# The last three token tiles of a fused attention, routing and MLP kernel in another order

## The chip, the core and the metric

The kernel runs on one core of one Trainium2 chip. The metric is the device time of one execution in microseconds (us). Before the change the median of three runs is 432.23 us (431.24 to 432.95).

## What is computed

Three stages follow one another in one launch. The first is a linear attention with decay over 2 x 768 tokens, 8 heads of 48 channels; its result is 1536 rows of 384. The second sends each row to the one of 8 experts with the largest gate logit, at most `capacity` rows each, and multiplies what the expert returns by a gate weight. The third is a dense MLP. Cut to what matters:

```python
state = w * state + k_t v_t^T                 # per head, token by token
y_t   = r_t @ (state_before + u * k_t v_t^T)
e     = argmax(x @ w_gate);  pos = rank of the token within its expert
disp[e, pos] = x                              # if pos < capacity
y     = relu(disp @ w1[e]) @ w2[e];  out = gate_w * y[e, pos]
g     = h * clip(h + 3, 0, 6) / 6,  h = out @ w_in;  result = g @ w_out
```

The gate weight is folded into the rows before they are dispatched (`sm` scales `x`), so a row is scaled once and then written to its expert's place.

## The kernel before

**Stages.** `attention()` (lines 242 to 886) walks 12 tiles of 128 tokens; `moe()` (line 897) walks the 8 experts, each with 224 columns of rows; `mlp()` (line 1084) walks blocks of 384 tokens. fp32 products of the two later stages are made of three products of a high and a low part: weights are cast to a high part on ScalarE (`high`, line 188) and the low part is a subtraction (`low`, line 194).

**Order.** The scheduler is manual: each engine runs its instructions in the order in which the Python code issues them, and semaphores join the engines. The small steps of the routing of a tile stand in a list `todo`; `tick(n)` issues the next n of them on VectorE (with a ScalarE or GpSimd instruction inside some), `ranks(0)` issues the rank products on TensorE, `gate(t)` the logits, `turn(t)` three transposes on TensorE and the copy `xT` on ScalarE that `gate` reads, `values(t, i)` eight products, `finish_x(t, i)` the addition on VectorE (line 435) that completes half of a tile's rows, `bonus(t)` eight scalings on ScalarE (line 429) that this addition needs.

**Routing of a tile** (`route`, line 588): maximum, one-hot, exponent; then `ranks`; sum and reciprocal (`inverse`, line 616), the position, and `done` (line 639). Tiles 9, 10 and 11 (`t >= LATE`) do not go through DRAM for expert 0: their rows are put into expert 0's tile by products with a selection matrix. For that `inverse` makes a high part `lasth` on ScalarE (line 620), a low part `lastl` is made by VectorE (line 632, tiles 9 and 11) or GpSimd (line 625, tile 10), and `done` makes the selection `first` (line 642). `late_rows(t)` (line 677) then issues six products: three with the high part, three with the low part. All three tiles are also scattered to DRAM by an indirect DMA of GpSimd (`spread`, line 702) for the other experts; `fetch(e)` (line 234) reads an expert's rows back and waits for all the scatters before it.

**Zero products.** `keep_warm(n, bank)` (line 254) issues n bf16 products of a tile of zeros, 128x384; nothing reads them.

**The end of the stage** (lines 828 to 886) is written out by hand: tile 11's attention, the routing of tiles 9, 10 and 11 interleaved, 12 products that bring expert 0's fetched rows `xr` into the same PSUM tiles (line 877), `late_rows`, and then `moe()` begins with `turn(0)`, whose copies `xh` (line 923) start expert 0's first products (line 995). In the iteration for tile 10 the piece of expert 0's weights that covers its second half is cast on ScalarE by `high(slice(0, PC))` (line 820).

Of the kernel before, what the change touches and what calls it, by code (L numbers as in the profile page):

```python
# [8 lines left out]
F32 = mybir.dt.float32  # L9
F32R = mybir.dt.float32r  # L10
# [3 lines left out]
ALU = mybir.AluOpType  # L14
# [51 lines left out]
def kernel(  # L66
# [175 lines left out]
    def attention():  # L242
        actx = ExitStack()
        with actx:
# [159 lines left out]
            def carried(T):  # L404
                py_t[T] = [
                    (bank(2 + i, "py") if T < NTILE - 1 else bank("a", "py"))[:, :DM].rearrange(
                        "p (n i d) -> p n i d", n=NP, i=2
                    ) for i in range(2)
                ]
                if T % CB:  # L410
                    for p in range(NP):
                        for i in range(2):
                            nc.tensor.matmul(  # L413
                                py_t[T][i][:, p], head(rT[T], i)[:, p, :],
                                head(Z[T], i)[:, p, :].unsqueeze(1).to_broadcast([D, 2, D]),
                                start=p == 0, stop=False,
                            )
# [8 lines left out]
            def bonus(T):  # L426
                x_t[T] = xq.tile([P, DM], F32, tag="x", name="x")
                for h in range(H):
                    nc.scalar.activation(
                        x_t[T][:, h * D:(h + 1) * D], v_of(T)[:, h % 2, h // 2, :], AF.Copy, scale=dg[T][:, h]  # L430
                    )
# [29 lines left out]
            def turn(T):  # L461
                pt = bank("tr", "pt")[:, :DM].rearrange("p (k t) -> p k t", k=KD)
                for k in range(KD):
                    nc.tensor.transpose(pt[:, k, :], x_t[T][:, k * P:(k + 1) * P], ident)  # L464
                xT = p2.tile([P, KD, P], F32, tag="xT", name="xT", bufs=1)
                nc.scalar.copy(xT, pt)
                xT_t[T] = xT
# [21 lines left out]
            def ranks(age=1):  # L489
                if todo and isinstance(todo[0][0], list):  # L490
                    age_, mm = todo[0][0]
                    if age_ >= age:
                        todo[0].pop(0)
                        mm()
                    else:
                        todo[0][0][0] += 1
# [91 lines left out]
            def route(t):  # L588
                if t < GRP * NGRP:
                    if t % GRP == GRP - 1:  # L590
                        route_group(t - GRP + 1)
                    return
                last, tail = t >= LATE, t == NTILE - 1
                pl = lgt.pop(t)
                l, po = pl[:, 0:E], pl[:, 64:64 + 2 * E]
                rk, pe = pl[:, 192:192 + E], pe_all[:, t, :]
                oh = oh_all[:, t, :]
                oh2 = oh.unsqueeze(1).to_broadcast([P, 2, E])
                slot = slots[:, t:t + 1]
                V = nc.vector  # L600
                mx = p2.tile([P, 1], F32, tag="mx", name="mx")
                d = p2.tile([P, E], F32, tag="d", name="d")
                m2 = p2.tile([P, 1], F32, tag="m2", name="m2")
                sm = p2.tile([P, 1], F32, tag="sm", name="sm", bufs=4)
                sel = p2.tile([P, 2, E], F32, tag="sel", name="sel")
                sf = p2.tile([P, 1], F32, tag="sf", name="sf")

                def diff():
                    V.tensor_tensor(out=d, in0=l, in1=mx.to_broadcast([P, E]), op=ALU.subtract)
                    nc.scalar.activation(gex[:, t % GRP, 0:E], d, AF.Exp)  # L610

                def rank_mm():
                    base_mm(po, t, True, False)
                    nc.tensor.matmul(po, tri, oh2, start=False, stop=True)

                def inverse():
                    V.reciprocal(sm, sm)
                    if last:
                        hi = lastp.tile([P, DM], F32R, name=f"lasth{t}")
                        nc.scalar.activation(hi, x_t[t], AF.Copy, scale=sm)  # L620
                        last_h[t] = hi
                        if t == NTILE - 2:
                            nc.scalar.activation(x_t[t], x_t[t], AF.Copy, scale=sm)
                            lo = lastp.tile([P, DM], F32R, name=f"lastl{t}")
                            nc.gpsimd.tensor_tensor(out=lo, in0=x_t[t], in1=hi.bitcast(F32), op=ALU.subtract)
                            last_l[t] = lo

                def low_rows():
                    o = first[t]
                    if t != NTILE - 2:  # L630
                        lo = lastp.tile([P, DM], F32R, name=f"lastl{t}")
                        V.scalar_tensor_tensor(
                            out=lo, in0=xs_t[t], scalar=sm, in1=last_h[t].bitcast(F32), op0=ALU.mult, op1=ALU.subtract
                        )
                    else:
                        lo = last_l[t]
                    first[t] = ((last_h[t], o), (lo, o))

                def done():
                    if last:  # L640
                        o = lastp.tile([P, WIN], F32R, name=f"first{t}")
                        V.tensor_scalar(
                            out=o, in0=col, scalar1=sf, scalar2=None, op0=ALU.is_equal
                        )
                        first[t] = o
                        xs_t[t] = x_t[t]
                        last_ops[t] = [low_rows]
                    V.tensor_scalar(out=slot, in0=sf, scalar1=float(FAR), scalar2=None, op0=ALU.add)
                    if t == NTILE - 2:
                        ready.append((slot, x_t.pop(t)))  # L650
                    else:
                        scat.append((slot, x_t.pop(t), sm))

                todo.append([
                    lambda: V.tensor_reduce(out=mx, in_=l, axis=AX.X, op=ALU.max),
                    lambda: V.scalar_tensor_tensor(
                        out=rk, in0=l, scalar=mx, in1=rank, op0=ALU.is_equal, op1=ALU.mult
                    ),
                    diff,
                    lambda: V.tensor_reduce(out=m2, in_=rk, axis=AX.X, op=ALU.max),  # L660
                    lambda: V.tensor_tensor(out=oh, in0=rk, in1=m2.to_broadcast([P, E]), op=ALU.is_equal),
                    [0, rank_mm],
                    lambda: V.tensor_reduce(out=sm, in_=gex[:, t % GRP, :], axis=AX.X, op=ALU.add),
                    inverse,
                    lambda: V.tensor_tensor(
                        out=sel, in0=po.rearrange("p (a e) -> p a e", a=2), in1=oh2, op=ALU.mult
                    ),
                    lambda: V.tensor_reduce(out=pe.unsqueeze(2), in_=sel, axis=AX.X, op=ALU.add),
                    lambda: V.tensor_scalar(
                        out=sf, in0=pe[:, 0:1], scalar1=cap_f, scalar2=pe[:, 1:2], op0=ALU.is_lt, op1=ALU.mult  # L670
                    ),
                    done,
                ])

# [72 lines left out]
            for T in range(NTILE - 1):  # L747
# [69 lines left out]
                    rest = low  # L817
                if T == 10:
                    high, low = begin(hi_only=True)
                    high(slice(0, PC))  # L820
                finish_x(T, 0)
                finish_x(T, 1)
                if T == 10:
# [8 lines left out]
            fetch(0)  # L832
            load_to(7)
            T = NTILE - 1
            carried(T)
            bonus(T)
            values(T, 0)
            ranks(0)
            turn(T - 1)
            finish_x(T, 0)  # L840
            drain(0)
            values(T, 1)
            gate(T - 1)
            finish_x(T, 1)
            load_to(8)
            keep_warm(2, 0)
            route(T - 1)
            tick(3)
            turn(T)
            tick(2)  # L850
            finish(T - 2)
            late_rows(LATE, 0)
            keep_warm(2, 0)
            ranks(0)
            keep_warm(3, 0)
            tick(5)
            gate(T)
            route(T)
# [10 lines left out]
            tick(2)  # L869
            drain(0)  # L870
            finish(T)
            scale()
            scatter()
            keep_warm(3, 0)
            for n in range(2 * KD):
                k, c = divmod(n, 2)
                nc.tensor.matmul(
                    px0[k][:, c * P:min(WIN, (c + 1) * P)], xr[:, c, k * P:(k + 1) * P],
                    ident[:, :min(P, WIN - c * P)], start=False, stop=False,
                )  # L880
            late_rows(LATE + 1)
            late_rows(T)
            scatter()
            scale(nc.vector)
            scatter()
            late.extend((lambda: rest(nc.vector, slice(HC, PC)), lambda: low(nc.vector)))
# [549 lines left out]
```

## Time and profile before

| | |
|---|---|
| median of 3 runs | 432.23 us (431.24 to 432.95) |
| the profiled execution | 431.22 us |
| its span, first to last instruction | 429.4 us |
| mean granted TensorE clock over the span | 0.985 |
| TensorE busy | 416.0 us (97%), 3159 products |
| VectorE / ScalarE / GpSimd busy | 251.8 / 204.1 / 177.0 us |
| first product of the experts (line 995) | 90.28 us after the start |

The profiled execution has its own time; the 1.8 us between it and the span lie ahead of the first and behind the last instruction. Times of rows are counted from the start of the span. A granted clock of 1.00 is 2.4 GHz and 0.50 is 1.2 GHz.

### The profile page before, as it was taken

How to read it: one execution, taken by the hardware profiler on the slowest of the kernel's cores; microseconds unless marked ns; L12 is line 12 of the kernel's file. 1: busy time of each engine (PE TensorE's matmuls, PEld its weight loads, DVE VectorE, ACT ScalarE, POOL GpSimd, SP SyncE). 2: the span in 40 equal slices, each digit the busy share in tenths (PEclk: the TensorE clock that was granted, in tenths of full speed). 3: DMA queues.
4: the chain of work that ended last, by engine and by line, in shares of the span. 5: the costliest groups of instructions: out<-in, count | busy, mean ns of one | idle time of the engine just before them, and what ended most of it. 6: DMA issues, size and time to landing. Idle time of an engine off the chain costs nothing.

```text
span 429.4 us, 8115 instructions
## 1 busy us (share of the span) xinstructions
PE 416.0 (97%) x3159; PEld 403.1 (94%) x3159; DVE 251.8 (59%) x473; ACT 204.1 (48%) x434; POOL 177.0 (41%) x146
## 2 busy tenths in 40 slices
PE   7999999899999999999999999999999999999992
PEld 4799999799999999999999999999999999999992
DVE  5998988598986767775978779670313122130310
ACT  2374677556636656658436254352505134250520
POOL 4875685126567467567000000001625226160441
PEclk9999999699999999999999999999999999999997
DMA  7987999646198899898622511001010000100001
GB/s 225 234 272 265 334 338 393 226 143 279 50 288 255 195 352 255 198 358 211 232 76 73 173 65 60 0 2 55 2 37 20 0 2 0 56 1 2 0 21 44
DMA packets 17361, 62.20 MB, mean 145 GB/s; under 512 B 2912, under 2 KB 7136, under 8 KB 17312
## 3 DMA queue, kind: packets, MB, share of 16 engines
q1 hardware_dynamic: 13024, 54.27, 40.1%
q0 software_dynamic: 1968, 4.73, 3.1%
q10 hardware_dynamic: 2320, 2.57, 1.8%
q8 instruction: 27, 0.44, 0.4%
q14 instruction: 22, 0.18, 0.1%
HBM read 53.70 MB, written 7.87 MB: 143 GB/s over the span
## 4 chain that ended last, share of the span: by engine, by line
PE 85%; issue 6%; POOL 2%; DMA 2%; DVE 2%; ACT 1%; SPq 0%; POOLq 0%; DVEq 0%; ACTq 0%
PE psh L1113 20%; PE pso L1136 19%; PE psm L995 15%; PE pym L1030 6%; PE pym L1034 6%; PE py L421 4%; PE pym L1031 3%; PE psa L394 2%; PE pl L475 2%; DMA hTt<-in_hT_dram 2%; PE py L413 2%; POOL gl L1102 2%; PE pt L464 1%; PE pu L442 1%; PE px L913 1%
## 5 line engine op out<-in xcount | busy, mean ns | idle before, releaser
L1117 DVE SCALAR_TENSOR_TENSOR g<-g,psh 128x384 f32<-128x384 f32 x64 | 35.3, 552 | 98.8 <-ACT g L1116 98.4
L1116 ACT ACTIVATE g<-psh,three 128x384 f32<-128x384 f32 x64 | 37.2, 582 | 73.3 <-PE psh L1113 73.3
L1102 POOL TENSOR_TENSOR gl<-g,gh 128x384 fp32r<-128x384 f32 x40 | 40.3, 1012 | 51.1 <-ACT gh L1101 51.1
L1154 POOL DMA_INDIRECT out_dram<-o,cid x12 | 11.8, 980 | 116.2 <-ACT o L1152 107.9
L1030 PE MATMUL pym<-h,wbh 128*128 128x448 f32 x120 | 38.3, 377 | 0.0
L194 POOL TENSOR_TENSOR wal<-raw,wah 128x1536 fp32r<-128x1536 f32 x7 | 24.6, 3517 | 24.4 <-ACT wah L188 12.9
L1101 ACT CAST gh<-g 128x384 fp32r<-128x384 f32 x64 | 32.3, 505 | 3.5 <-DVE g L1117 3.5
L1001 ACT ACTIVATE h<-psm 128x448 fp32r<-128x448 f32 x32 | 17.5, 547 | 32.3 <-PE psm L995 31.6
L1113 PE MATMUL psh<-y2l,wbh 128*128 128x384 f32 x96 | 32.4, 337 | 0.0
L1113 PE MATMUL psh<-y2l,wah 128*128 128x384 f32 x96 | 32.4, 337 | 0.0
L1113 PE MATMUL psh<-y2h,wah 128*128 128x384 f32 x96 | 32.3, 336 | 0.0
L1113 PE MATMUL psh<-y2h,wbh 128*128 128x384 f32 x96 | 32.3, 336 | 0.0
L1113 PE MATMUL psh<-y2h,wbl 128*128 128x384 f32 x96 | 32.1, 335 | 0.0
L1113 PE MATMUL psh<-y2h,wal 128*128 128x384 f32 x96 | 32.1, 335 | 0.0
L1136 PE MATMUL pso<-wah,gh 128*128 128x384 f32 x96 | 32.1, 334 | 0.0
L1136 PE MATMUL pso<-wbh,gh 128*128 128x384 f32 x96 | 32.1, 334 | 0.0
L1136 PE MATMUL pso<-wbh,gl 128*128 128x384 f32 x96 | 32.1, 334 | 0.0
L1136 PE MATMUL pso<-wal,gh 128*128 128x384 f32 x96 | 32.1, 334 | 0.0
L1136 PE MATMUL pso<-wah,gl 128*128 128x384 f32 x96 | 32.1, 334 | 0.0
L1136 PE MATMUL pso<-wbl,gh 128*128 128x384 f32 x96 | 32.1, 334 | 0.0
L995 PE MATMUL psm<-xh,wah 128*128 128x224 f32 x192 | 31.9, 275 | 0.1
L995 PE MATMUL psm<-xh,wal 128*128 128x224 f32 x192 | 31.7, 275 | 0.0
(192 smaller groups left out, 1143.6 us busy)
## 6 DMA issues: line engine op xcount, KB each, us to landing
raw<-in_w_dram SPq DMA_DIRECT2D x32, 768.0 KB, 8.2
tokt<-in_tok_dram SPq DMA_DIRECT2D x12, 576.0 KB, 4.7
raw<-in_w_in_dram SPq DMA_DIRECT2D x8, 768.0 KB, 5.0
raw<-in_w_out_dram SPq DMA_DIRECT2D x8, 768.0 KB
hTt<-in_hT_dram SPq DMA_DIRECT2D x12, 448.0 KB, 5.6
xs<-zero SPq DMA_DIRECT2D x8, 384.0 KB
xr<-xs ACTq DMA_DIRECT2D x6, 384.0 KB, 7.6
xr<-xs SPq DMA_DIRECT2D x2, 384.0 KB, 3.2
```

The lines of the kernel that those rows point to most:

```text
L194: eng.tensor_tensor(out=lo[:, sl][:, h], in0=raw[:, h], in1=hi[:, sl][:, h].bitcast(F32), op=ALU.subtract)
L421: nc.tensor.matmul(py_t[T][i][:, p], A_t[T % 2][:, i, p, :], v_of(T)[:, :, p, :], start=T % CB == 0 and p == 0, stop=p == NP - 1,)
L995: nc.tensor.matmul(ps[:, fi, :], wa_tile(a, k, 2 * q + fi), b[:, k, :], start=n == k == 0 and not (both and fi), stop=n == 2 and k == KD - ...
L1001: nc.scalar.activation(hh, ps, AF.Relu)
L1030: nc.tensor.matmul(py[k], w2h[:, w], h2, start=f == 0, stop=False)
L1034: nc.tensor.matmul(py[k // 2][:, k % 2, :], a[:, w], h2[:, i], start=n == 0, stop=n == 3 * NF - 1)
L1101: nc.scalar.copy(gh, g)
L1102: (nc.vector if any(do) else nc.gpsimd).tensor_tensor(out=gl, in0=g, in1=gh.bitcast(F32), op=ALU.subtract)
L1113: nc.tensor.matmul(ps, wa_tile(a, k, f), y, start=n == 0, stop=n == 3 * KD - 1)
L1116: nc.scalar.activation(g, ps, AF.Relu, bias=three)
L1117: nc.vector.scalar_tensor_tensor(out=g, in0=g, scalar=6.0, in1=ps, op0=ALU.min, op1=ALU.mult)
L1136: nc.tensor.matmul(po, a[:, sl], c[:, wo], start=(h == 0 or (b, s) in acc) and f == 0 and n == 0, stop=(h == 1 or defer) and f == NF - 1 a ...
```

## The change

Within `route`: tile 9's rows are scaled in place by ScalarE and its low part is made by GpSimd, as those of tile 10 already were, but only when `finish(9)` is called; tile 11 alone keeps the VectorE form. The slot numbers of tiles 9 to 11 are computed by GpSimd. At the end of the stage: the cast of the weight piece moves from tile 10's iteration to behind tile 11's `finish`; `bonus(11)` is issued ahead of `carried(11)`; the rank products of tile 9 and `turn(10)` are issued ahead of `values(11, 0)`, with 4 and 3 zero products around them; tile 9 is scattered right behind its `finish`; three zero products behind `ranks` of tile 10 go, one of two ahead of `turn(11)` goes, and of the three ahead of the `xr` products two are left; `late_rows(10)` goes ahead of the `xr` products. Counted in these lines there are 15 zero products after the change and 13 before.

```diff
+                def scaled():
+                    x = xs_t.get(t) or x_t[t]
+                    nc.scalar.activation(x, x, AF.Copy, scale=sm)
+                    lo = lastp.tile([P, DM], F32R, name=f"lastl{t}")
+                    nc.gpsimd.tensor_tensor(out=lo, in0=x, in1=last_h[t].bitcast(F32), op=ALU.subtract)
+                    last_l[t] = lo
...
                         if t == NTILE - 2:
-                            nc.scalar.activation(x_t[t], x_t[t], AF.Copy, scale=sm)
-                            lo = lastp.tile([P, DM], F32R, name=f"lastl{t}")
-                            nc.gpsimd.tensor_tensor(out=lo, in0=x_t[t], in1=hi.bitcast(F32), op=ALU.subtract)
-                            last_l[t] = lo
+                            scaled()
...
-                    if t != NTILE - 2:
+                    if tail:
...
-                        last_ops[t] = [low_rows]
-                    V.tensor_scalar(out=slot, in0=sf, scalar1=float(FAR), scalar2=None, op0=ALU.add)
-                    if t == NTILE - 2:
+                        last_ops[t] = [scaled, low_rows] if t == LATE else [low_rows]
+                    (nc.gpsimd if last else V).tensor_scalar(
+                        out=slot, in0=sf, scalar1=float(FAR), scalar2=None, op0=ALU.add
+                    )
+                    if last and not tail:
...
                     high, low = begin(hi_only=True)
-                    high(slice(0, PC))
...
             T = NTILE - 1
+            bonus(T)
             carried(T)
-            bonus(T)
+            keep_warm(4)
+            ranks(0)
+            keep_warm(3)
+            turn(T - 1)
+            tick(5)
             values(T, 0)
-            ranks(0)
-            turn(T - 1)
             finish_x(T, 0)
-            drain(0)
             values(T, 1)
+            finish_x(T, 1)
             gate(T - 1)
-            finish_x(T, 1)
+            tick(1)
             load_to(8)
-            keep_warm(2, 0)
+            keep_warm(1, 0)
+            turn(T)
             route(T - 1)
-            tick(3)
-            turn(T)
-            tick(2)
+            tick(5)
             finish(T - 2)
+            scatter()
             late_rows(LATE, 0)
             keep_warm(2, 0)
             ranks(0)
-            keep_warm(3, 0)
             tick(5)
             gate(T)
...
             finish(T)
-            scale()
             scatter()
-            keep_warm(3, 0)
+            high(slice(0, PC))
+            late_rows(LATE + 1)
+            keep_warm(2, 0)
...
-            late_rows(LATE + 1)
             late_rows(T)
-            scatter()
             scale(nc.vector)
             scatter()
```

## Rows read from the trace of the kernel before

**Rows 1.** The page: busy time, and the granted clock in 40 slices

```profile
PE 416.0 (97%) x3159; PEld 403.1 (94%) x3159; DVE 251.8 (59%) x473; ACT 204.1 (48%) x434; POOL 177.0 (41%) x146
...
PEclk9999999699999999999999999999999999999997
```

**Rows 2.** The chain that ended last, 70 to 96 us: start, length, what

```profile
77.48 0.37 DVE x L435
...
90.28 4.38 PE psm L995 x36
```

**Rows 3.** Timeline of TensorE: start, length, line, operation, [idle before <-releaser]

```profile
74.75 1.13 PE L421 MATMUL py<-tokt,A 128*128 128x96 f32 x8
...
77.90 0.55 PE L464 MATMUL pt<-ident,x 128*128 128x128 f32 x3 [1.74 <-DVE x L435]
78.28 1.64 PE L421 MATMUL py<-tokt,A 128*128 128x96 f32 x8
79.71 1.34 PE L475 MATMUL pl<-wg_sb,xT 128*128 128x8 f32 x6
80.90 0.80 PE L257 MATMUL psw<-zero 128*128 128x384 bf16 x2
...
83.68 1.12 PE L257 MATMUL psw<-zero 128*128 128x384 bf16 x3
84.59 1.09 PE L475 MATMUL pl<-wg_sb,xT 128*128 128x8 f32 x6
...
86.84 0.65 PE L257 MATMUL psw<-zero 128*128 128x384 bf16 x3
87.32 1.47 PE L877 MATMUL px<-ident,xr 128*128 128x128 f32 x12
88.58 0.57 PE L684 MATMUL px<-first,lasth 128*128 128x224 f32 x3
...
89.32 0.28 PE L684 MATMUL px<-first,lasth 128*128 128x224 f32 x1
```

**Rows 4.** Stretches of 1 us: busy by engine, then granted clock, DMA

```profile
78.00:79.00 1.00, 1.00 (x8) 1.00 (x9) 1.00 (x3) 1.00 (x4) 0.00 (x0) 0.76 0.00 0
...
82.00:83.00 1.00, 1.00 (x6) 0.86 (x5) 0.75 (x3) 0.57 (x2) 0.00 (x0) 0.50 0.89 350
...
85.00:86.00 1.00, 1.00 (x9) 0.98 (x9) 0.24 (x2) 0.00 (x0) 0.16 (x1) 0.83 0.46 191
```

**Rows 5.** Timeline of VectorE

```profile
77.48 0.36 DVE L435 TENSOR_TENSOR x<-py,x 128x192 f32<-128x192 f32 x1 [1.76 <-PE pl L614]
...
81.91 0.61 DVE L632 SCALAR_TENSOR_TENSOR lastl<-x,sm,lasth 128x384 fp32r<-128x384 f32 x1
...
85.72 0.17 DVE L655 TENSOR_REDUCE mx<-pl 128x1 f32<-128x8 f32 x1 [1.25 <-PE pl L475]
...
86.47 0.17 DVE L661 TENSOR_TENSOR oh_all<-pl,m 128x8 bf16<-128x8 f32 x1
```

**Rows 6.** Timeline of ScalarE

```profile
75.34 1.46 ACT L188 CAST wah<-raw 128x1536 fp32r<-128x1536 f32 x1
76.70 1.91 ACT L429 ACTIVATE x<-tokt,dg 128x48 f32<-128x48 f32 x8
78.53 0.48 ACT L466 COPY xT<-pt 128x384 f32<-128x384 f32 x1
...
87.76 0.60 ACT L693 ACTIVATE x<-x,sm 128x384 f32<-128x384 f32 x1
89.88 0.66 ACT L923 CAST xh<-px 128x224 fp32r<-128x224 f32 x2 [1.52 <-PE px L684]
```

**Rows 7.** Timeline of GpSimd (POOL), its start and 64 to 102 us

```profile
12.32 0.14 POOL L743 IOTA ids<- 128x12 int32 x1
...
84.17 0.99 POOL L625 TENSOR_TENSOR lastl<-x,lasth 128x384 fp32r<-128x384 f32 x1 [7.68 <-DVE pe_all L668]
87.22 0.99 POOL L703 DMA_INDIRECT xs<-x,slots  x1 [2.06 <-DVE sm L617]
```

## The prediction

> **What bounds the kernel now.** I read the page first. TensorE is busy for 97% of the span, and its clock is full in every slice but two, of which the one from 75.1 to 85.9 us is where the change lies [rows 1]. Then the chain of waits: from 90.28 us on it is products of the experts and of the MLP almost without a break [rows 2], so what the change is worth is how much sooner or later that first product of line 995 starts; the 339 us behind it I take as they are. The timeline of TensorE then shows what fills the time before it. TensorE waits 1.74 us, until 77.90, for VectorE's half of tile 10's rows (line 435) [rows 3]; VectorE itself had stood idle 1.76 us before that addition [rows 5]. By the code it waits for the products of `values(10, 1)`, whose last one should have ended near 73.9; the page names a later product as releaser. Why the release came only at 77.48 the trace does not show. Shortly after this gap the clock falls: 0.76 in the stretch of 78 to 79 us, 0.50 in that of 82 to 83, 0.83 again in that of 85 to 86 [rows 4]. So some 6.6 us, from about 78.8 to 85.3, run at 1.2 GHz. In that time TensorE has no idle time ahead of any step that I list: the transposes, `values(11, 1)`, `gate(10)`, the zero products and `gate(11)` follow each other [rows 3], while VectorE is idle 1.25 us for `gate(11)` [rows 5]. There each product costs its own length, zero products too.
>
> **What stays.** All that stands ahead of VectorE's addition at 77.48 on VectorE and TensorE is unchanged: the five scatters, the products of tile 10, the routing of tile 9 up to its one-hot. The change cannot release that addition earlier by anything I can name, since it waits only for products that come before the moved code. I therefore take 77.48 and the transposes at 77.90 as they are, and the fall of the clock behind them too. From there the change is a sum on TensorE.
>
> **The cast and `bonus`.** The cast of 1.46 us at 75.34 leaves ScalarE, so `bonus(11)` starts there and ends near 77.25 in place of 78.61. `xT` of tile 10 starts at 78.53, but its transposes end only at 78.45 [rows 3, 6], so the 1.36 us saved is spent waiting for TensorE: nothing. `bonus` ahead of `carried` is no move at all: they run on different engines. Where the cast goes, behind tile 11's high part, ScalarE now scales tile 9 (0.60 us at 87.76) and then waits 1.52 us for the `xh` copies [rows 6]. A cast from 87.76 ends at 89.22, before the 89.88 of `xh`: nothing as long as TensorE is not 0.7 us quicker there. Its low part follows on VectorE behind `xl`, as now.
>
> **The order on TensorE.** `values(11, 0)`, 0.97 us at full rate from its start at 74.75 (1.13 with its tail [rows 3]), filled the time ahead of the gap; now seven zero products fill it and are free, and `values(11, 0)` comes behind the transposes. The bounds of its price are 0.97 us at full rate and twice that, 1.94; `values(11, 1)`, which the clock caught in its first part, took 1.43 from 78.28 to 79.71 [rows 3]. I take 1.7, since two such steps now follow each other and the second is wholly at the low rate. Against that one zero product ahead of `turn(11)` goes (half of the 0.60 from 80.90 to the next step, 0.3) and three ahead of `gate(11)` go (0.91 from 83.68 to 84.59) [rows 3]. The sum so far is +1.7 - 0.3 - 0.9 = +0.5. `gate(11)` starts near 85.1 in place of 84.59 and its one-hot is ready near 87.1 in place of 86.6 (VectorE's five steps, 85.72 to 86.6 [rows 5]). Then one zero product at full rate goes: 0.48 / 3 = 0.16 (86.84 to 87.32 [rows 3]). That `late_rows(10)` comes before the twelve `xr` products is no more work, but they are asked for 1.7 us sooner (0.48 of zero products and 1.26 of `xr` [rows 3]), and that matters next.
>
> **GpSimd.** This is what the change makes late. GpSimd's instructions run in order, and now the three slot numbers, tile 9's low part and tile 9's scatter all stand there, the last two between tile 10's scaling and tile 10's low part. Slot numbers: no row shows such an operation of GpSimd; its smallest is 0.14 us (an iota, [rows 7]), and a full 384-wide one is 0.99, so 0.14 to 0.99 each. I take 0.14, as the width is one. The first falls in GpSimd's idle time of 7.68 us, the other two stand ahead of scatters that nothing waits for soon. Tile 9's low part: VectorE loses 0.61 us at 81.91 [rows 5], which is worth nothing since it waits afterwards, and GpSimd gains 0.99 [rows 7]. Its source must be scaled first (0.60 on ScalarE, the price of the row at 87.76 [rows 6]), and ScalarE gets there behind `xT` of tile 11. With `turn(11)` near 83.0 to 83.8, `xT` to 84.3 and the exponent of tile 10 (0.1), the scaling ends near 85.0, tile 9's low part near 86.0 (TensorE wants it then: nothing, or 0.1), the scatter (0.99, [rows 7]) near 87.1, and tile 10's low part, 84.17 to 85.16 now [rows 7], only near 88.1 to 88.4. TensorE has tile 11's ranks behind it at 87.3 and the high three products of `late_rows(10)` at 87.6. It then idles 0.5 to 0.8 us. I take 0.6. GPSIMD Engine Reference, section 4.1 (Engine selection), in the Trainium skill, puts a two-input elementwise operation at about twice VectorE's time on GpSimd, which speaks against this move. The rows have 0.99 against 0.61, a ratio of 1.6; by the rule the two low parts would take 1.22 us each, and the estimate of the wait would be 1.1 in place of 0.6.
>
> **Queues and DMAs.** SP's order stays: `fetch(1)` still waits for all three scatters. Tile 9's comes earlier, tiles 10's and 11's stand behind the late low part, so the last is issued near 90.3 (now 90.05 by the order of the three); what `fetch(1)` brings is wanted behind four blocks of expert 0, some 8 us later. VectorE loses three slot operations and one low part: it waits more, no more than that.
>
> **The sum.** +0.5 - 0.16 + 0.6 = +0.9 us. On the profiled execution (span 429.4, 431.22 with what lies around it) that gives 432.1. The median of the runs stands 1.0 above that execution, so I forecast 433.1. A change of 0.5% is 2.2 us, about what a measurement can tell from none: this is "the same".
>
> **Rivals.**
> 1. VectorE's late release does not come back. For: the page shows no cause, only a semaphore that came 3.5 us after its product should have ended, and four runs of one program differ by 1.7 us. Against: all before it is unchanged. Then the addition runs from 75.72, `turn(10)` from 76.2, and only now is the cast's removal worth something: `xT` from 77.25 to 77.7. Both `values` fill TensorE to 78.6, there is no gap, the clock stays, and `gate(10)` ends at 79.2 against 80.90 now. Scaling of tile 9 ends near 81.0, and GpSimd's row of low part, scatter and low part (0.99 + 0.99 + 0.3 of issue + 0.99) ends at 84.3; then 0.34 for the low three products, 0.32, 1.26 and 0.96 from the start of `late_rows(11)` at 89.32 to 90.28 [rows 2, 3]: line 995 starts at 87.2, 3.1 us sooner, 429.1. Chance 0.25.
> 2. As before, but TensorE's two waits for GpSimd there (0.8 and 0.9 us) take the clock down into the experts. 6.6 us at half rate, as now [rows 4], in a stretch bound by TensorE cost 3.3 and give it all back: 432.4. Chance 0.13.
> 3. The release is late, but the clock stays up over it. TensorE, Matmul & The Clock Gate in the Trainium skill, Part 1, says that the point of the change varies from run to run of one kernel; no run here shows that yet. From 77.90 at full rate the same order reaches line 995 near 89.0: 1.3 us sooner, 430.9. Chance 0.10.
> 4. Slower: the 0.6 us wait for tile 10's low part on GpSimd, so soon after the slow stretch, brings a second fall just as line 995 starts. It decides from the point where that wait, with the short one for tile 11's one-hot, is long enough; the 1.74 us of today was. Price +0.9 + 3.3 = +4.2 us, 436.4. For: GpSimd's queue gets 2.3 us longer. Against: the wait is a third of the one that did it. Chance 0.10.
>
> **How the numbers follow.** The forecast has 0.42, the rivals 0.25, 0.13, 0.10 and 0.10. Forecast, 2 and 3 are within 0.5%, rival 1 is faster, rival 4 slower; some of rival 1 may fall short and some of the forecast's upper bound (1.94 for `values`, 0.99 for each slot number ahead of the wait) pass over: 0.27, 0.61, 0.12. The range leaves out rival 4 and the far end of rival 1: 428.8 to 434.4. The likeliest case alone spans 432.4 to 434.2.
>
> **What would show it.** Right: TensorE still idle near 77 for line 435, zero products just ahead of it; a stretch of clock 0.50 of the same length; `gate(11)` 0.5 us later; GpSimd's line of low part, scatter, low part without a gap, and TensorE idle in front of the low half of `late_rows(10)` for GpSimd; `xh` unmoved by the cast. Wrong: VectorE's addition at once behind the one before it, a slice line with full clock through 75 to 86, or line 995 ahead of 89 us.

## The result and the profile after

| | before | after |
|---|---|---|
| time, median of 22 runs each, side by side | 431.69 us (427.75 to 434.88) | 434.94 us (432.16 to 439.07) |
| ratio, 95% interval | | 1.0077 (1.0054 to 1.0100) |
| a second series (35 and 12 runs) | 432.61 us | 434.57 us, 1.0040 (1.0012 to 1.0068) |
| profiled execution: time, span | 431.22, 429.4 us | 432.54, 430.7 us |
| first product of the experts | 90.28 us [rows 2] | 91.71 us |

The change makes the kernel slower, by 0.8% in one series and 0.4% in the other; forecast were 433.1 us, a range up to 434.4 and "the same". Single executions differ by more than that, mostly with TensorE's clock, so each kernel below is given with its **time at half rate**: twice its span times what its mean granted clock lacks of 1, averaged over its runs. It counts every stretch at 1.2 GHz, the last microseconds of the span with them. The ratios leave out slow runs (over 1.5% above a kernel's fastest) and the means take in all runs; without the slow ones the changed kernel's 14.5 us at half rate would be 13.8, the 11.4 of before 10.8, and the 12.4 of experiment 1 8.9.

The page of the changed kernel: busy time of the engines, the granted clock in 40 slices.

```profile
PE 414.0 (96%) x3161; PEld 402.4 (93%) x3161; DVE 255.0 (59%) x469; ACT 203.7 (47%) x434; POOL 179.0 (42%) x150
...
PEclk9999999899999999999999999999999999999998
```

The slice that stood at 6 [rows 1] stands at 8: this execution was at half rate for a shorter time, and yet came out 1.3 us longer. Stretches of 1 us of the changed kernel: busy by engine, then granted clock, DMA share, GB/s.

```profile
79.00:80.00 1.00, 1.00 (x8) 0.98 (x6) 0.93 (x5) 0.09 (x1) 0.00 (x0) 0.59 0.02 8
80.00:81.00 1.00, 1.00 (x6) 1.00 (x6) 0.42 (x2) 0.90 (x2) 0.23 (x1) 0.50 0.00 0
...
82.00:83.00 1.00, 1.00 (x9) 1.00 (x8) 0.00 (x0) 0.00 (x0) 0.00 (x0) 0.71 1.13 385
83.00:84.00 1.00, 1.00 (x10) 1.00 (x11) 0.90 (x4) 0.00 (x0) 0.00 (x0) 1.00 1.02 276
...
88.00:89.00 1.00, 0.37 (x4) 0.34 (x3) 0.86 (x4) 1.00 (x1) 1.00 (x3) 1.00 0.60 238
```

The clock lacks 0.41, 0.50, 0.50 (the row between) and 0.29 of four stretches: 3.4 us at 1.2 GHz. The same sum over the kernel before is 0.24, six times 0.50 and 0.17, so 6.8 us ([rows 4] has three of the stretches; the prediction said 6.6). In the last row, at full clock, TensorE is busy for 37% and GpSimd for all of it. Timeline of TensorE in the changed kernel:

```profile
75.28 0.82 PE L257 MATMUL psw<-zero 128*128 128x384 bf16 x4
...
78.59 0.65 PE L257 MATMUL psw<-zero 128*128 128x384 bf16 x3 [1.97 <-remote]
79.08 0.74 PE L464 MATMUL pt<-ident,x 128*128 128x128 f32 x3
79.61 3.35 PE L421 MATMUL py<-tokt,A 128*128 128x96 f32 x16
...
84.69 0.82 PE L475 MATMUL pl<-wg_sb,xT 128*128 128x8 f32 x6
86.37 0.59 PE L690 MATMUL px<-first,lastl 128*128 128x224 f32 x3 [0.85 <-POOL lastl L620]
...
88.66 0.59 PE L690 MATMUL px<-first,lastl 128*128 128x224 f32 x3 [0.63 <-POOL lastl L620]
...
91.71 1.02 PE L1001 MATMUL psm<-xh,wah 128*128 128x224 f32 x6
```

TensorE gets to tile 11 at 75.28 us, where it was 74.75 [rows 3], with nothing changed ahead of it. From there to the first expert product it takes 16.43 us, 0.90 more than the 15.53 of before. That is the sum of the prediction, but of other terms: 1.48 us of waits for GpSimd, 3.4 us less of half rate, and 0.28 us more from VectorE's addition to the transposes (78.38 to 79.08, before 77.48 to 77.90), because three of the seven zero products came only behind the stall. Behind the first expert product the span goes on for 339.0 us, before for 339.1. VectorE's late release came back (the kernel of before had it at 77.48 [rows 5]; `remote` is a releaser that the profile cannot name):

```profile
76.24 0.35 DVE L435 TENSOR_TENSOR x<-py,x 128x192 f32<-128x192 f32 x1
78.38 0.36 DVE L435 TENSOR_TENSOR x<-py,x 128x192 f32<-128x192 f32 x1 [1.79 <-remote]
```

GpSimd's timeline in the changed kernel, where before there was one low part and a gap [rows 7]:

```profile
80.55 0.23 POOL L652 TENSOR_SCALAR slots<-sf 128x1 int32<-128x1 f32 x1 [3.39 <-DVE sf L675]
85.33 0.99 POOL L620 TENSOR_TENSOR lastl<-x,lasth 128x384 fp32r<-128x384 f32 x1 [4.54 <-ACT x L618]
86.48 1.08 POOL L709 DMA_INDIRECT xs<-x,slots  x1 [0.16 <-POOL lastl L620]
87.59 1.02 POOL L620 TENSOR_TENSOR lastl<-x,lasth 128x384 fp32r<-128x384 f32 x1
88.56 0.81 POOL L652 TENSOR_SCALAR slots<-sf 128x1 int32<-128x1 f32 x2
```

The chain that ended last runs through it, piece by piece (start, length, what), where before it was TensorE's own products up to 85.7 us, and then steps of VectorE and ScalarE for tile 11:

```profile
85.33 1.00 POOL lastl L620
...
86.48 1.08 POOL xs L709
...
87.59 1.03 POOL lastl L620
...
88.66 0.59 PE px L690 x3
```

ScalarE shows the cast hidden, as forecast: it ends at 89.07, and `xh` waits for TensorE after it.

```profile
87.61 1.46 ACT L188 CAST wah<-raw 128x1536 fp32r<-128x1536 f32 x1
91.31 0.66 ACT L929 CAST xh<-px 128x224 fp32r<-128x224 f32 x2 [2.24 <-PE px L690]
```

### The profile page after: what moved, and what is told of

It reads as the page before. It is cut to its first block, busy times and chain, and to the rows that moved or that the text cites. A ratio compares the mean times of both kernels' runs of the same rounds, so it can differ in the third digit from the quotient of the medians.

```text
span 430.7 us, 8119 instructions
## 1 busy us (share of the span) xinstructions
PE 414.0 (96%) x3161; PEld 402.4 (93%) x3161; DVE 255.0 (59%) x469; ACT 203.7 (47%) x434; POOL 179.0 (42%) x150
## 4 chain that ended last, share of the span: by engine, by line
PE 80%; issue 7%; DVE 4%; POOL 3%; DMA 2%; ACT 1%; another core or an unknown queue 0%; SPq 0%; POOLq 0%; DVEq 0%; ACTq 0%
PE psh L1119 20%; PE pso L1142 19%; PE psm L1001 15%; PE pym L1036 6%; PE pym L1040 6%; PE py L421 3%; PE pym L1037 3%; DMA hTt<-in_hT_dram 2%; POOL gl L1108 2%; PE psa L394 2%; PE py L413 1%; PE pl L475 1%; PE px L919 1%; PE pu L442 1%; PE pt L464 1%
## 5 line engine op out<-in xcount | busy, mean ns | idle before, releaser
L1007 ACT ACTIVATE h<-psm 128x448 fp32r<-128x448 f32 x32 | 17.5, 547 | 32.6 <-PE psm L1001 31.9
```

Source lines behind the costliest of these rows:

```text
L1007: nc.scalar.activation(hh, ps, AF.Relu)
```

## The experiments

All are measured beside the kernel before, which had 131 runs in four series, 11.4 us at half rate on the mean. Where a kernel was run twice, both ratios stand.

| kernel | median, us | ratio to before (95%) | us at half rate |
|---|---|---|---|
| changed kernel, twice | 434.94; 434.57 | 1.0077 (1.0054 to 1.0100); 1.0040 (1.0012 to 1.0068) | 14.9; 13.8 |
| GpSimd's part undone, twice | 432.68; 433.72 | 1.0022 (0.9985 to 1.0059); 0.9989 (0.9954 to 1.0025) | 10.1; 14.6 |
| tile 9's scatter later, twice | 435.91; 432.40 | 1.0100 (1.0052 to 1.0149); 0.9992 (0.9957 to 1.0028) | 19.4; 12.1 |
| order undone | 433.53 | 1.0068 (1.0034 to 1.0102) | 13.5 |
| cast alone | 433.25 | 1.0027 (0.9995 to 1.0058) | 12.5 |
| GpSimd waits filled, twice | 433.67; 435.61 | 1.0069 (1.0031 to 1.0107); 1.0025 (0.9986 to 1.0065) | 12.8; 14.8 |
| seven zero products first | 434.08 | 1.0050 (1.0019 to 1.0080) | 15.0 |
| fourteen first | 431.93 | 1.0014 (0.9982 to 1.0045) | 10.0 |
| fourteen first, GpSimd's part undone | 430.49 | 0.9981 (0.9946 to 1.0016) | 5.1 |
| before with nine zero products, twice | 429.14; 429.33 | 0.9956 (0.9925 to 0.9987); 0.9940 (0.9912 to 0.9968) | 5.9; 4.7 |
| the same with cast and GpSimd's part | 431.14 | 0.9994 (0.9962 to 1.0025) | 6.0 |
| before without five scatters | 428.05 | 0.9933 (0.9901 to 0.9966) | 8.9 |

A common slope fitted over all runs of these kernels and of before, the last line's left out, is 0.35 us of time for 1 us at half rate (standard error 0.01). It separates, roughly, what a part costs at an equal clock from what the clock adds: taken kernel by kernel the slope runs from 0.08 to 0.53.

**1. GpSimd's part undone:** tile 9's low part back on VectorE, its scatter at the end. The slot numbers stay on GpSimd, and the cast stays moved.

```diff
-                    if tail:
+                    if t != NTILE - 2:
...
-                        last_ops[t] = [scaled, low_rows] if t == LATE else [low_rows]
+                        last_ops[t] = [low_rows]
...
-                    if last and not tail:
+                    if t == NTILE - 2:
...
             finish(T - 2)
-            scatter()
...
             finish(T)
+            scale()
             scatter()
...
             late_rows(T)
+            scatter()
```

> The changed kernel with tile 9's low part back on VectorE and its scatter back at the end, so that GpSimd has nothing ahead of tile 10's low part. Theory 1 (GpSimd's queue: TensorE waits 0.85 and 0.63 us for low parts, line 620, and these waits also let the clock fall in some runs): both waits are gone, and most of the 3.2 us come back, ratio to the kernel before 1.003 or less. Theory 2 (the order on TensorE: values(11, 0) behind the transposes and zero products that wait, so that the clock is lost longer): at most 1.5 us come back, ratio 1.005 or more.

432.68 us against 434.94. In its profile one wait for GpSimd is left, 0.20 us, the idle 1.96 us ahead of the transposes is still there, and the clock stayed up. Run again:

> The changed kernel with GpSimd's part undone, again. If GpSimd's part is what makes the time at half rate longer, this one has about 10 us of it on the mean beside 15 of the changed kernel, and 432 to 433 us. If the idle stretch of TensorE ahead of the transposes, which both have, decides it alone, it has 13 to 16 us as the changed kernel has, and 433 to 434 us: shorter only by the two waits for GpSimd.

433.72 us, 14.6 us at half rate: this time the clock was no better than the changed kernel's (13.8 in the same series). At an equal time at half rate it is 0.4 us ahead of the changed kernel (432.69 and 433.12 at 10 us, standard errors 0.20 and 0.17), which is not clear of noise.

**2. Only the place of tile 9's scatter:** behind tile 10's low part.

```diff
             finish(T - 2)
-            scatter()
             late_rows(LATE, 0)
...
             late_rows(T)
+            scatter()
             scale(nc.vector)
```

> The changed kernel with tile 9's scatter behind tile 10's low part on GpSimd. Tile 9's low part stays on GpSimd. Theory 1: the second wait (0.63 us for tile 10's low part) is gone, the first (0.85 us) stays; 1 to 2 us come back, ratio 1.003 to 1.005. Theory 2: under 0.6 us, ratio about 1.007.

A miss, 435.91 us: its profile is at half rate from 77.6 to 94.6 us, and TensorE, that slow, waits for GpSimd nowhere. Again:

> The changed kernel with tile 9's scatter behind tile 10's low part, again: the first time it had six runs and the most time at half rate of all, 19 us on the mean, though TensorE waited for GpSimd not once in its profile. If GpSimd's order ahead of the low parts matters for the clock, it is again above the changed kernel; if that was chance, it has 13 to 16 us, as the changed kernel, and 434 to 435 us.

432.40 us and 12.1 us at half rate: the 19 us of those six runs did not come back. At an equal time at half rate it is 0.7 us ahead of the changed kernel (432.39 at 10 us, standard error 0.23), where the scatter, 1.08 us long, stood ahead of tile 10's low part.

**3. Order undone:** TensorE's old order and zero products, GpSimd's part and the cast kept.

```diff
-            keep_warm(4)
+            values(T, 0)
             ranks(0)
-            keep_warm(3)
             turn(T - 1)
-            tick(5)
-            values(T, 0)
             finish_x(T, 0)
+            drain(0)
             values(T, 1)
             gate(T - 1)
...
-            keep_warm(1, 0)
-            turn(T)
+            keep_warm(2, 0)
             route(T - 1)
...
+            turn(T)
```

> The changed kernel with the old order from bonus(11) to finish(9) and the old zero products there; tile 9's low part, its scatter and the cast stay as changed. Theory 1: the waits for GpSimd stay or grow, ratio 1.005 or more. Theory 2: most of it comes back, ratio 1.003 or less.

433.53 us: the old order does not take the loss away, though in its profile TensorE, at half rate, waits for GpSimd nowhere. Its 13.5 us at half rate (standard error 0.9) are not those of before either. There both of VectorE's additions for tile 10 ran back to back and the transposes waited for nothing, but then TensorE itself stood still among the products of `values(11, 1)`, with nothing that the profile shows to wait for (`issue`), and at 80.6 us the clock fell:

```profile
75.34 0.53 PE L464 MATMUL pt<-ident,x 128*128 128x128 f32 x3
...
76.32 0.45 PE L421 MATMUL py<-tokt,A 128*128 128x96 f32 x2 [0.38 <-issue]
77.76 0.70 PE L421 MATMUL py<-tokt,A 128*128 128x96 f32 x5 [0.99 <-issue]
```

**4. The cast alone,** moved in the kernel before.

```diff
                     high, low = begin(hi_only=True)
-                    high(slice(0, PC))
...
             finish(T)
             scale()
             scatter()
+            high(slice(0, PC))
```

> The kernel before with the cast alone moved behind tile 11's rows. Both theories: bonus(11) ends 1.36 us earlier, the transposes still wait for VectorE's addition at about 77.5, so nothing: ratio 0.998 to 1.002. If the late release of that addition were caused by the cast, it would come up to 1.7 us earlier and the kernel would be faster by 0.4 to 1%.

433.25 us, an interval around 1: inconclusive as to a cost, and no gain. At an equal time at half rate it stands 0.5 us above the kernel before (432.00 at 10 us, standard error 0.28), so a small cost is not excluded, and experiments 1, 2, 3, 5, 6 and 8 all have the cast moved. VectorE's addition waits 1.79 us again, so the cast was not what released it late.

**5. The two waits for GpSimd filled** with zero products, in the changed kernel.

```diff
             tick(5)
+            keep_warm(5, 0)
             late_rows(LATE, 1)
...
-            late_rows(LATE + 1)
+            late_rows(LATE + 1, 0)
+            keep_warm(5, 0)
+            late_rows(LATE + 1, 1)
             keep_warm(2, 0)
```

> The changed kernel with ten more zero products: five ahead of the low half of the low rows of tile 9, where TensorE idled 0.85 us for GpSimd, and five between the high and the low products of tile 10's rows, where it idled 0.63 us. At 0.16 us each at full rate they about fill the two waits. Theory 1 (the two waits for GpSimd cost their own length and also keep the clock down or bring it down again): the waits' idle time becomes busy time, the first expert product moves by less than 0.3 us, but the time at half rate gets shorter, from 14.9 us on the mean of the runs to about 10, and the time falls by 1 to 2 us, to 433 to 434. Rival A (the waits cost only their own length, and the length of the half-rate stretch has nothing to do with them): time at half rate as in the changed kernel, 435 to 435.6. Rival B (zero products at half rate are themselves in the way): slower by up to 1.6 us, 435.5 to 436.6.

> The changed kernel with ten zero products in TensorE's two waits for GpSimd, again. If the idle time in these waits is what keeps the clock at half rate for longer, it has 9 to 11 us at half rate, as the kernel with GpSimd's part undone; if not, 13 to 16 us, as the changed kernel.

12.8 us at half rate, then 14.8: over 24 runs 13.8 (standard error 1.3), against 14.5 (0.9) over the changed kernel's 34. On the mean, idle time in those two waits isn't what keeps the clock down.

**6. The zero products in one group,** seven of them (the diff), and in a second kernel fourteen, `keep_warm(14)` in the same place.

```diff
-            keep_warm(4)
+            keep_warm(7)
             ranks(0)
-            keep_warm(3)
             turn(T - 1)
```

> The changed kernel with its seven zero products in one group ahead of the ranks, none added. In the changed kernel the second group of three waited for a semaphore of the first. If that wait is what lengthens the idle stretch, seven in one group do nearly what fourteen did: 432 to 433. If it is only the number of products that fills the stretch, TensorE still idles some 1.5 us for VectorE and the time stays near the changed kernel's, 434 to 435.

> The changed kernel with its seven zero products ahead of the transposes of tile 10 made into fourteen in one group, ahead of the ranks. In the changed kernel the second group waited 1.97 us for a semaphore of the first group, and TensorE stood idle in that time; in one group there is no such wait and fourteen products at 0.16 us fill 2.2 us of it. If it is this idle stretch after which the clock falls, it should fall less often or for less long: time at half rate from 14.9 us on the mean to under 8, the time down by 2 us, to about 433. If VectorE's late release alone sets the time there and the clock falls for other reasons (what comes later, at GpSimd), nothing changes: 434.5 to 435.5. In both, VectorE's addition for tile 10 still comes near 78.4 us.

Seven first change nothing (434.08, 15.0 us); with fourteen it is 431.93 and 10.0 us, by the ratios 1.6 us less than with seven. So it is not the second group's wait for the first but the length of the idle stretch. With seven first TensorE stands idle 2.09 us for VectorE, at full clock in this execution:

```profile
79.97 0.55 PE L464 MATMUL pt<-ident,x 128*128 128x128 f32 x3 [2.09 <-DVE x L435]
...
85.69 0.59 PE L690 MATMUL px<-first,lastl 128*128 128x224 f32 x3 [0.85 <-POOL lastl L620]
...
87.97 0.59 PE L690 MATMUL px<-first,lastl 128*128 128x224 f32 x3 [0.63 <-POOL lastl L620]
...
91.03 1.02 PE L1000 MATMUL psm<-xh,wah 128*128 128x224 f32 x6
```

**7. The kernel before with nine zero products** in its own idle stretch.

```diff
             values(T, 0)
+            keep_warm(9)
             ranks(0)
             turn(T - 1)
```

> The kernel before with nine zero products put behind the first products of values(11), where TensorE idled 1.74 us for VectorE (1.4 us of products at full rate). If the idle stretch is what the clock's fall follows, the time at half rate falls from 10.9 us on the mean of the runs to under 5 and the time by 2 us, to about 429.5 to 430: a kernel ahead of both. If not, 431.5 to 432.2. It leaves all of GpSimd's part as it was before, so beside the changed kernel with its products in one group it tells how much the clock can bring in either order.

> The kernel before with nine zero products once more, on this chip beside the three others: 428.7 to 429.8 us, 0.3 to 0.9% faster than the kernel before, time at half rate about 6 us on the mean of the runs against about 11.

It is ahead of both kernels, twice. In the first run's profile VectorE's release is as late as ever (77.02 us, after 2.48 us of waiting), the transposes start no sooner than before (77.73 against 77.90 [rows 3]), but no idle stretch lies ahead of them and the clock stays at 2.4 GHz:

```profile
75.13 0.88 PE L257 MATMUL psw<-zero 128*128 128x384 bf16 x4
76.26 0.32 PE L257 MATMUL psw<-zero 128*128 128x384 bf16 x1 [0.24 <-issue]
76.98 0.81 PE L257 MATMUL psw<-zero 128*128 128x384 bf16 x4 [0.40 <-issue]
...
77.73 0.53 PE L464 MATMUL pt<-ident,x 128*128 128x128 f32 x3
...
87.20 0.37 PE L996 MATMUL psm<-xh,wah 128*128 128x224 f32 x1
```

From the transposes to the experts it takes 9.47 us, before 12.38 (90.28 - 77.90). In the second run's profile VectorE's two additions for tile 10 ran back to back and TensorE stood still by itself instead, for 0.82 us ahead of its last rank product; the clock stayed up there too, and it took 9.28 us:

```profile
75.41 0.74 DVE L435 TENSOR_TENSOR x<-py,x 128x192 f32<-128x192 f32 x2
...
78.69 0.17 PE L614 MATMUL pl<-oh_all,tri 128*128 128x16 bf16 x1 [0.82 <-issue]
```

**8. The price of each part with the clock up.** The kernel of 7 with cast and GpSimd's part, and the changed kernel with fourteen products first and GpSimd's part undone; their diffs are those of 3, 7 and of 1, 6 together.

> The kernel before with nine zero products behind values(11,0), plus the cast and all of GpSimd's part of the change (slot numbers, tile 9's low part, its scatter early). Against the kernel before with nine zero products (429.1 us) it tells the price of GpSimd's part while the clock is up. Theory 2: TensorE waits for GpSimd twice, by 0.6 to 0.9 us each, in front of the low half of tile 9's and of tile 10's rows, and the time is 1.2 to 1.7 us longer, 430.4 to 430.9. Rival C: no wait of weight at full clock, 429 to 429.5. Rival D: the waits bring the clock down again, 432 and more.

> The changed kernel with both undone at once: tile 9's low rows back on VectorE with its scatter at the end, and fourteen zero products in one group ahead of the transposes of tile 10. Theory 2 (the change loses twice: 1.5 us in TensorE's two waits for GpSimd, whatever the clock, and about as much by the idle stretch of its second group of zero products, after which the clock falls for longer): the order itself costs nothing, the first expert product starts near 87.2 to 87.7 us, the time comes out at the 429 to 430 us of the kernel before with nine zero products. Rival C (the two are one loss: GpSimd's waits hurt only because the clock is low, or the other way round): undoing the second brings nothing more, 431.5 to 432.5.

With GpSimd's part but not the order 431.14 us, 1.8 above the 429.33 of the same series; with the order but not GpSimd's part 430.49, 1.2 above. Both are above what was expected (430.4 to 430.9, and 429 to 430), so the order is not free. Both have the cast moved and the slot numbers on GpSimd. TensorE with GpSimd's part:

```profile
80.03 0.53 PE L464 MATMUL pt<-ident,x 128*128 128x128 f32 x3
...
85.24 0.59 PE L690 MATMUL px<-first,lastl 128*128 128x224 f32 x3 [0.56 <-POOL lastl L620]
...
87.51 0.59 PE L690 MATMUL px<-first,lastl 128*128 128x224 f32 x3 [0.61 <-POOL lastl L620]
...
90.57 1.02 PE L1001 MATMUL psm<-xh,wah 128*128 128x224 f32 x6
```

TensorE with the order:

```profile
80.15 0.52 PE L464 MATMUL pt<-ident,x 128*128 128x128 f32 x3
...
86.23 0.17 PE L512 MATMUL pl<-cum,ones 128*128 128x16 bf16 x1 [0.30 <-DVE oh_all L667]
...
87.33 0.59 PE L690 MATMUL px<-first,lastl 128*128 128x224 f32 x3 [0.20 <-POOL lastl L620]
...
90.39 1.12 PE L1001 MATMUL psm<-xh,wah 128*128 128x224 f32 x6
```

From the transposes to the experts at full clock: 9.47 us with neither, 10.54 with GpSimd's part, 10.24 with the order, 11.06 with both (seven first). So GpSimd's part costs 1.1 there, the order 0.8, both 1.6, each read from one profile; the two profiles with neither differ by 0.2. The run times do not confirm every one of these: at an equal time at half rate fourteen first stand at 432.33 with GpSimd's part and at 432.36 without (standard errors 0.28). With the idle stretch filled, the waits for GpSimd (0.56 and 0.61) do not bring the clock down: 6.0 us at half rate against 5.9 and 4.7.

**9. Where the late release comes from:** the kernel before without the five scatters of tile 10's iteration (the first change in the diff stands twice, and a third `scatter()` of the second goes likewise).

```diff
                 if T >= 6:
-                    scatter()
+                    skip(T) if T == 10 else scatter()
...
                     drain(1)
                     scale()
-                    scatter()
-                    scatter()
+                    skip(T)
+                    skip(T)
...
+            def skip(t):
+                if ready:
+                    ready.pop(0)
```

> The kernel before without the five scatters that GpSimd issues back to back in the iteration of tile 10 (70.3 to 76.5 us); their rows are not written, so the experts get other data. It asks where VectorE's late release at 77.48 us comes from: TensorE's semaphores are updated late between 72 and 78.5 us, in the time of these scatters. If the scatters' transfers delay the semaphores, VectorE's addition for tile 10 comes near 75.7 us instead of 77.48, the idle 1.74 us of TensorE goes, the clock stays up and the first expert product starts 3 to 4 us sooner: 427 to 428.5. If the delay comes from something else (TensorE's own instruction stream, the weight loads), the addition comes near 77.5 us again and the time stays within 1 us of the kernel before, 431 to 432.

Both additions for tile 10 run back to back, and the next wait is another:

```profile
74.37 0.61 DVE L435 TENSOR_TENSOR x<-py,x 128x192 f32<-128x192 f32 x2
74.89 0.95 DVE L194 TENSOR_TENSOR wal<-raw,wah 128x768 fp32r<-128x768 f32 x1
77.41 0.36 DVE L435 TENSOR_TENSOR x<-py,x 128x192 f32<-128x192 f32 x1 [1.56 <-ACT x L429]
```

428.05 us, and its profile has the clock up. This is one profile, but the 17 profiles with the scatters bear it out. In 14 of them the late addition starts 0.99 to 1.22 us behind the end of the fifth scatter. Here are the fifth scatters of the kernel before (it ends at 76.49, the addition starts at 77.48) and of the changed kernel (77.16, 78.38):

```profile
75.52 0.97 POOL L703 DMA_INDIRECT xs<-x,slots  x1 [0.30 <-issue]
...
76.19 0.97 POOL L709 DMA_INDIRECT xs<-x,slots  x1 [0.30 <-issue]
```

In the other three (experiment 3, fourteen first, the second run of 7) the additions were not late, and TensorE itself stood still until 0.79 to 0.83 us behind that end. TensorE's idle stretch goes with how far it is ahead of that end when it is through with tile 10: 1.74 us ahead before, 1.88 in the changed kernel, 2.50 in the first profile of experiment 5, and idle for 1.74, 1.97 and 2.94. So the late release hangs on those scatters. By what path (their descriptors, their writes, their completion) no run here tells.

## Why the prediction was wrong

**What held.** VectorE's late release came back; the cast is hidden in the profile; the four zero products that run ahead of the stall cost nothing (the other three ran behind it and were not free); the 339 us behind the first expert product stayed; GpSimd's line of low part, scatter, low part stands without a gap, and TensorE waits 0.63 us for tile 10's low part (0.6 forecast, 0.5 to 0.8).

**The step that failed: "I therefore take 77.48 and the transposes at 77.90 as they are, and the fall of the clock behind them too."** The stretch at half rate is no fixed length of this program. Over its runs the kernel before had 3.4 to 20.9 us of it in one series of 35; one trace showed 6.8, and I took that as given. What goes with it in most of these kernels is the idle stretch of TensorE ahead of the transposes. Where that is left as the change makes it (1.94 to 2.94 us in the profiles), the mean is 12.4 to 15.0 us in five kernels, against 11.4 with the 1.74 us of before; where zero products fill it, 4.7 to 6.0 in three kernels, and 10.0 in the fourth, whose profile has its half rate in another stage, between 10 and 33 us (slices 2 and 3 of the granted clock at 6 and 8). The changed kernel has 14.5 over its 34 runs, 3.1 more than before, and 0.35 x 3.1 = 1.1 us. That these 3.1 us come from the longer idle stretch is likely, but not shown: the old order (experiment 3) had 13.5 us as well, and the cast alone 12.5. The change makes that stretch longer in two ways: only four of its zero products fill it (0.65 us, where `values(11, 0)` took 0.97), since the second group waits along with the transposes; and the addition came 3.10 us behind tile 10's last products (75.28 to 78.38; with seven first 3.07), where it had been 2.73 (74.75 to 77.48 [rows 3, 5]). TensorE: Matmul & The Clock Gate in the Trainium skill, Part 1, says of the rise at the start of sustained products that its point varies from run to run of one kernel. Of the falls in mid-kernel these runs show such a variation too, 17.5 us at half rate between two runs of one program.

**The sum's two mis-sized terms.** At an equal time at half rate the changed kernel stands 1.6 us above the kernel before (433.12 and 431.48 at 10 us), where I had 0.9. With the 1.1 of the clock that is the 2.7 by which the means of all runs differ (434.72 and 431.98). First, the low part of tile 9: forecast "nothing, or 0.1", measured 0.85 of waiting in the changed kernel, 0.56 with the old order. I had set GpSimd's times against a TensorE that was at half rate until 85.3. GpSimd doesn't slow with that clock: a low part takes 1.00 us in the run of experiment 2 that was at half rate, and 0.99 here. In this execution TensorE was back at full rate at 82.6 us, reached the low rows sooner, and what the clock gave back was spent on waiting. In the changed kernel's second profile, where TensorE is at half rate from 87.7 us on, it does not wait for tile 10's low part at all. A wait for a fixed-speed engine and a slow clock do not add; the sum needs both cases. Second, the order: 0.34 forecast with products at half rate; at full rate the products alone come to +0.1 (1.92 - 1.03 for `values`, less five zero products of 0.16), but 0.8 was measured. Of that 0.30 is a wait for tile 11's one-hot (VectorE came to it straight from tile 10's steps, where with the old order it had stood idle for 0.39 us before it), and 0.20 one for tile 10's low part: the twelve `xr` products and three zero products had covered the latter, and the change puts the `xr` products behind it. I had seen that they were asked for sooner, and put it all on GpSimd's longer queue. The remaining 0.2 is no more than the two profiles with neither part differ by.

**Rivals.** Rival 1 (no late release) did not happen in the changed kernel's two profiles. With fourteen zero products first it did, and TensorE stood still by itself for 0.80 us. Experiment 9 shows its premise: without the scatters VectorE waits 1.56 us for `bonus`, and there the cast's move could pay; no run tried it. Rival 3 (late release, full clock) is what single executions show: experiment 1's first profile (430.36 us) and seven first (431.65 us). Rival 4 had the right sign, and its second fall does occur, but behind the wait for tile 9's low part, which I had put at nothing. In the changed kernel's second profile (436.81 us) the clock is back at 84.3 us, falls again at 87.7 during the wait of 0.85 us, and stays at half rate until 94.6. The fall and the row behind it, and the wait:

```profile
87.00:88.00 1.00, 0.15 (x3) 0.06 (x2) 0.86 (x7) 0.97 (x3) 0.91 (x1) 0.87 0.92 375
88.00:89.00 1.00, 1.00 (x4) 0.85 (x5) 0.62 (x4) 0.44 (x3) 0.93 (x1) 0.50 0.24 88
...
87.97 0.98 PE L690 MATMUL px<-first,lastl 128*128 128x224 f32 x3 [0.85 <-POOL lastl L620]
```

In the changed kernel's first profile, with seven first and in experiment 8 such waits brought no fall, and filling them did not change the mean by more than its error (experiment 5). Two profiles cannot tell whether its chance of 0.10 was too low. What also moved the mean, a longer first fall, stood in no rival.

**What stays open:** how much of the 12.4 us of GpSimd's part undone (10.1 and 14.6) against 14.5 is more than chance; how often the waits for GpSimd bring a second fall; why the old order with GpSimd's part and the cast had 13.5; and how the scatters delay TensorE's release.

## What to carry over

Before costing a reordering around a stall, find out whether the clock falls behind that stall in every run or only in some: a stretch at half rate in one trace is a draw, and in most of these kernels its mean length went with the idle stretch ahead of it. Filling that stretch gained something where the reordering lost: nine zero products took 0.4 to 0.6% off the kernel before. And work moved to an engine whose speed doesn't follow TensorE's clock has to be set against TensorE at full rate, where it has the least time to hide.

## What was not expected

- One program on one chip had 3.4 to 20.9 us at half rate in 35 runs, and times of 428.15 to 436.51 us go with it: 0.35 us for each of those microseconds, not 0.5. That fits with waits of TensorE that get shorter while it is slow.
- Zero products are not always issued back to back: among nine in a row TensorE stood 0.24 and 0.40 us with nothing that the profile shows to wait for, in the same time in which VectorE's release is late.
- A slot number of one column took GpSimd 0.23 us alone and 0.81 for two in the changed kernel, 0.54 for two in experiment 1's first profile; the low part took 0.99 there and 0.61 on VectorE, as before.
